# Attention and gated FFN on one core: the bias of 36 steps added by TensorE, their minima by one reduce, and an add moved from ScalarE to GpSimd

## The chip, the cores and the metric

The kernel runs on one core of one Trainium2 chip. A core has TensorE (PE; its weight loads are shown as PEld), VectorE (DVE), ScalarE (ACT), GpSimd (POOL) and SyncE (SP, which here only issues DMAs). Each works through its own queue in order and waits on semaphores of the others. The metric is the device time of one execution in microseconds; lower is better.

## The reference

```python
scores = scale * np.matmul(q, k.transpose(0, 1, 3, 2))          # scale = 1/8
keep = is_global | is_local                                     # 8 global keys, 96 local ones
bias = -slopes[:, None, None] * dist[None, :, :]                # slope 2**-(head+1)
scores = np.where(keep, scores + bias[None], -1e9)
a = np.exp(scores - np.max(scores, axis=-1, keepdims=True))
a = a / (np.sum(a, axis=-1, keepdims=True) + 1e-09)
x = np.matmul(a, v)                                             # B=4, H=8, S=768, D=64
h = np.maximum(x @ w_in, 0.0)                                   # 512 -> 1024
conv = sum(conv_w[t] * shifted(h, t) for t in range(3))
out = (h * (1 / (1 + np.exp(-conv)))) @ w_out                   # 1024 -> 512
```

Only keys inside the window can count, so a tile of 128 queries needs 96 earlier keys, its own 128 and 8 global ones: 232 columns, or 136 for the first tile of a sequence.

## The kernel before

The work is cut into 32 jobs: 4 batches, 2 halves of the sequence (384 queries each), 4 pairs of heads. A job is 3 steps, one for each tile of 128 queries, so there are 96 steps, numbered s = 0 to 95. A step computes both heads of a pair:

- `scores` (L368): q times k on TensorE into PSUM. Jobs 0 to 8 (`NATIVE = 9`, `BESIDE = 9`; steps 0 to 26) multiply in fp32, one head on rows 0 to 63 of the array and the other on rows 64 to 127, line L384. The first head's result goes to a tile named `s`, the second's to one named `sb` from another pool. Later jobs use two split matmuls for each head, line L394, both heads in one bank.
- `maxima` (L402): for each head one DVE instruction, L411, multiplies the scores by -0.125, adds the table `tab` of negated bias and mask (bf16, SBUF), writes the sum back to PSUM and gives its minimum; a short second instruction reads that accumulator.
- `exps` (L416): for each head an Exp on ScalarE with that minimum and a sum, L425. For steps under `SHARED = 40` ScalarE then adds 1e-9 to both sums, L431.
- `normalise` (L433): DVE takes the reciprocals (L437; from step 40 on it also does the add, L436). Up to step 39 GpSimd scales one head (L443) and ScalarE the other (L441).
- `transposes` two steps later (L451, evicted by ScalarE at L453), `values` at the end of a job (L469), and `mixed` (L481, L482), which splits the attention output into two parts for the FFN.

Beside that run: the decode of the weights, which come as 64-bit words, in 16 pieces (DVE L315, L317, L319 and L330, a cast on GpSimd L324, four raw buffers, so a new piece is loaded when an old one has been decoded); the split of q and k for jobs from 9 on (`prep`: casts on GpSimd L136 and L137, subtractions on DVE L140 and L141); and the FFN of the unit before: first matmul `mm1` (L500, L521), convolution (GpSimd L546, DVE L547 and L548), gate, second matmul `mm2` (L611).

Steps 0 to 10 (`HAND = 11`) stand in the order in which the code is written. There DVE gets a budget of decode work for each step, `DECODE_BY_HAND`, later `DECODE_LATER`. From step 11 on a scheduler with a simulated timeline orders each engine's queue, so that an instruction can also be put into a queue's earlier places. Loads of q, k, v and weights share SP's queue. Warm-up matmuls (L169) keep TensorE's clock up in the hand steps.

Of the kernel before, what the change touches and what calls it, by code (L numbers as in the profile page):

```python
# [66 lines left out]
def fast_path(tc, io):  # L67
# [56 lines left out]

    def prep(m, part):
        if m >= len(jobs) or m < NATIVE:
            return
# [243 lines left out]
    def scores(s):  # L371
# [6 lines left out]
        both = ps_s.tile([P, 2, 256], F32, tag="s", name=f"s{s}")  # L378
        sp = [both[:, 0], bank(f"sb{s}", True) if m < BESIDE else both[:, 1]]
        for j in range(2):  # L380
            if m < NATIVE:
# [7 lines left out]
                    stop=True,  # L389
# [3 lines left out]
            for n_, (q_, st, sp_) in enumerate(((qh, True, False), (ql, False, True))):  # L393
# [652 lines left out]
```

## Time and profile before

| | |
|---|---|
| median of 3 runs | 463.97 us (452.75 to 464.49) |
| the profiled execution | 452.65 us, span 450.7 us |
| PE busy | 434.5 us, 96% of the span |
| DVE busy | 351.9 us, 78% |
| ACT busy | 304.0 us, 67% |
| POOL busy | 225.8 us, 50% |
| TensorE's granted clock, mean | 0.995 |

The span runs from the first to the last instruction of the profiled execution. A matmul's duration in the profile holds its way through the array, so the next one starts before it ends, and a busy PE is not a PE at its peak. The same holds in a smaller measure for DVE and ACT: an instruction's shown end can lie behind the next one's start.

### The profile page before, as it was taken

To read this page: it belongs to the slowest core of one execution; us is meant where nothing else is said; L and a number is where in the kernel's file an instruction comes from. 1 tells how busy PE (TensorE), PEld (TensorE's weight loads), DVE (VectorE), ACT (ScalarE), POOL (GpSimd) and SP (SyncE) were. 2 spreads that over 40 slices of the span, in tenths; PEclk is the share of its full clock that TensorE was granted. 3 is DMA by queue.
4 is the path that set the end of the run, shared out by engine and by line. 5 is a ranking of instruction groups with operands and counts; after the bars stand their busy time and mean duration, and the time that the engine had idled before them with its cause. 6 is when DMAs were issued, how large, how long until landed. Compare 5 with 4: busy or idle time off the path is not lost.

```text
span 450.7 us, 9020 instructions
## 1 busy us (share of the span) xinstructions
PE 434.5 (96%) x3027; PEld 375.6 (83%) x3027; DVE 351.9 (78%) x927; ACT 304.0 (67%) x839; POOL 225.8 (50%) x315
## 2 busy tenths in 40 slices
PE   8789999999889999999999999999999999998997
PEld 6555678899768988899989988889989988798876
DVE  6899998889989877757989897847989986447800
ACT  3778878788799667647776576646775696547610
POOL 5654446637835472656675585646675651022000
PEclk9989999999999999999999999999999999999999
DMA  6979941343244332353234333442335223584111
GB/s 213 306 221 275 279 121 43 108 147 105 83 129 150 108 107 97 92 166 107 86 120 160 107 108 91 130 138 81 106 119 163 81 83 119 207 293 132 47 49 52
DMA packets 22662, 60.02 MB, mean 133 GB/s; under 512 B 3024, under 2 KB 5584, under 8 KB 22608
## 3 DMA queue, kind: packets, MB, share of 16 engines
q1 hardware_dynamic: 18992, 53.01, 38.1%
q10 hardware_dynamic: 3616, 6.36, 3.8%
q8 instruction: 26, 0.43, 0.4%
q14 instruction: 28, 0.23, 0.2%
HBM read 53.07 MB, written 6.29 MB: 132 GB/s over the span
## 4 chain that ended last, share of the span: by engine, by line
PE 73%; DVE 5%; ACT 4%; DMA 4%; POOL 2%; issue 2%; ACTq 0%; POOLq 0%; DVEq 0%
PE o L611 24%; PE h L500 24%; PE pv L469 7%; PE t L451 7%; PE s L394 6%; DMA check<-in_w 3%; DVE c L547 1%; PE last L632 1%; POOL pbuf L443 1%; PE sb L384 1%; PE s L384 1%; DVE c L548 1%; DVE c L599 1%; ACT pbuf L425 1%; ACT sat L577 1%
## 5 line engine op out<-in xcount | busy, mean ns | idle before, releaser
L443 POOL TENSOR_SCALAR pbuf<-pbuf,mm 128x232 f32<-128x232 f32 (+1 forms) x152 | 109.1, 726 | 74.1 <-DVE mm L437 49.2
L425 ACT ACTIVATE pbuf<-s,mm 128x232 f32<-128x232 f32 (+1 forms) x165 | 72.5, 444 | 37.6 <-DVE mm L411 22.8
L411 DVE CUSTOM_DVE_ANT_0 s<-s,tab 128x232 f32<-128x232 f32 (+1 forms) x165 | 63.1, 384 | 24.9 <-PE s L394 21.8
L546 POOL TENSOR_SCALAR c<-hbuf,cw 128x382 f32<-128x382 f32 (+1 forms) x64 | 50.0, 786 | 59.3 <-ACT hbuf L510 59.3
L611 PE MATMUL o<-woh,gh 128*128 128x512 f32 x184 | 74.0, 402 | 0.0
L611 PE MATMUL o<-wol,gh 128*128 128x512 f32 x184 | 73.2, 398 | 0.0
L611 PE MATMUL o<-woh,gl 128*128 128x512 f32 x184 | 73.2, 399 | 0.0
L451 PE MATMUL t<-ident,pbuf 128*128 128x128 f32 x384 | 63.0, 278 | 6.6 <-ACT pbuf L441 3.7
L453 ACT ACTIVATE pt<-t 128x512 f32<-128x512 f32 x96 | 58.0, 604 | 15.4 <-PE t L451 15.3
L451 PEld LDWEIGHTS t<-ident,pbuf 128*128 128x128 f32 x384 | 45.5, 141 | 19.6 <-ACT pbuf L441 5.1
L500 PE MATMUL h<-xh,wih 128*128 128x384 f32 x252 | 58.1, 345 | 1.7 <-ACT hbuf L510 1.2
L500 PE MATMUL h<-xl,wih 128*128 128x384 f32 x252 | 58.8, 342 | 0.0
L500 PE MATMUL h<-xh,wil 128*128 128x384 f32 x252 | 56.3, 340 | 0.0
L469 PE MATMUL pv<-pt,v 128*64 128x128 f32 (+1 forms) x768 | 50.0, 279 | 0.3 <-ACT pt L453 0.3
L469 PEld LDWEIGHTS pv<-pt,v 128*64 128x64 f32 (+1 forms) x768 | 42.3, 138 | 8.9 <-issue 2.5
L500 PEld LDWEIGHTS h<-xh,wih 128*128 128x128 f32 x252 | 42.9, 189 | 4.1 <-ACT hbuf L510 1.9
L547 DVE SCALAR_TENSOR_TENSOR c<-hbuf,cw,c 128x382 f32<-128x382 f32 (+1 forms) x64 | 43.7, 697 | 3.0 <-POOL c L546 2.7
L500 PEld LDWEIGHTS h<-xh,wil 128*128 128x128 f32 x252 | 44.2, 189 | 0.3 <-issue 0.3
L500 PEld LDWEIGHTS h<-xl,wih 128*128 128x128 f32 x252 | 44.0, 189 | 0.2 <-issue 0.2
L548 DVE SCALAR_TENSOR_TENSOR c<-hbuf,cw,c 128x382 f32<-128x382 f32 (+1 forms) x64 | 43.4, 686 | 0.3
L510 ACT ACTIVATE hbuf<-h 128x384 f32<-128x384 f32 x64 | 31.9, 500 | 17.4 <-PE h L500 17.0
L611 PEld LDWEIGHTS o<-woh,gl 128*128 128x128 f32 x184 | 34.7, 188 | 7.7 <-issue 0.2
(119 smaller groups left out, 846.6 us busy)
## 6 DMA issues: line engine op xcount, KB each, us to landing
v<-in_vv SPq DMA_DIRECT2D x32, 384.0 KB, 3.7
rq<-in_qk SPq DMA_DIRECT2D x23, 384.0 KB, 3.1
wr<-in_w SPq DMA_DIRECT2D x16, 512.0 KB, 5.2
check<-in_w SPq DMA_DIRECT2D x16, 512.0 KB, 4.6
rk<-in_qk SPq DMA_DIRECT2D x12, 504.0 KB, 3.6
out<-ob ACTq DMA_DIRECT2D x23, 256.0 KB, 2.1
rk<-in_qk SPq DMA_DIRECT2D x11, 408.0 KB, 3.2
rq<-in_qk SPq DMA_DIRECT2D x16, 96.0 KB, 4.4
```

What stands on the lines that cost most here:

```text
L411: last_ttr[s] = V.tensor_tensor_reduce(out=sp[j][:, c0 : c0 + n], in0=sp[j][:, c0 : c0 + n], in1=tb, scale=-0.125, scalar=3.0e38, op0=ALU. ...
L425: last_exp[s] = A.activation(pb[:, j, c0 : c0 + n], sp[j][:, c0 : c0 + n], AF.Exp, bias=mm[:, j : j + 1], scale=-1.0, accum_out=mm[:, 2 + ...
L443: G.tensor_scalar(x, x, inv, 1.0, ALU.mult, ALU.mult)
L451: T.transpose(pt[:, j, c, :], pb[:, j, c * P : (c + 1) * P], ident)
L453: last_ev[s] = A.activation(sb, pt, AF.Copy)
L469: T.matmul(pv[m][64 * j : 64 * j + 64, i * P : (i + 1) * P], vt[m][:n, i, c, 64 * j : 64 * j + 64], sb[:n, j, c, :], start=c == 0, stop=c ...
L500: T.matmul(ps[:, :TB], w_[:, k, fs], x_, start=part == 0 and k == 0, stop=part == 2 and k == NK - 1,)
L510: A.activation(half, ps[:, :TB], AF.Relu, scale=0.5)
L546: G.tensor_scalar(c, *tap(1), 1.0, ALU.mult, ALU.mult)
L547: V.scalar_tensor_tensor(c, *tap(0), c, ALU.mult, ALU.add)
L548: V.scalar_tensor_tensor(c, *tap(2), c, ALU.mult, ALU.add)
L611: last = T.matmul(ps, g_[:, f], w_[:, f], start=f == 0 and part == 0, stop=f == NF - 1 and part == 2,)
```

## The change

Jobs 1 to 12 (`BIASED = (1, 13)`, steps 3 to 38) get their bias from TensorE: after the score matmuls of a head a further one, with a bf16 identity scaled by -0.125 as weights and the table as the moving operand, adds to the same PSUM columns. Since -0.125 is in the weights there, q is multiplied by -0.125 first: for jobs 1 to 8 by a new GpSimd instruction over 128 x 384 in place, for jobs 9 to 12 inside the instructions of `prep`. DVE then takes the minima of both heads with one `tensor_reduce`, which writes nothing back.

For the first 27 steps both heads' scores lie in one tile of two banks (pool `ps_w`, two buffers); at step 27 that pool is given up for the narrow tiles. The add of 1e-9 for steps 0 to 39 is GpSimd's. The decode budgets grow.

```diff
+BIASED = (1, 13)
-DECODE_BY_HAND, DECODE_LATER = (0.3, 1.2, 1.4), (1.2, 1.2)
+DECODE_BY_HAND, DECODE_LATER = (0.3, 1.5, 1.8), (1.6, 1.6)
@@ prep
+        if m < NATIVE and biased(m) and part == 0:
+            q = raw[m][0][:, :TB]
+            G.tensor_scalar(q, q, -0.125, 1.0, ALU.mult, ALU.mult)
...
-            G.tensor_copy(qh, rq)
+            if biased(m):
+                G.tensor_scalar(qh, rq, -0.125, 1.0, ALU.mult, ALU.mult)
+            else:
+                G.tensor_copy(qh, rq)
...
+                V.scalar_tensor_tensor(ql, rq, -0.125, qh.bitcast(F32), ALU.mult, ALU.subtract)
@@ tables
+    A.activation(ident16, ident, AF.Copy, scale=-0.125)
@@ scores
-        both = ps_s.tile([P, 2, 256], F32, tag="s", name=f"s{s}")
-        sp = [both[:, 0], bank(f"sb{s}", True) if m < BESIDE else both[:, 1]]
+        if m < BESIDE:
+            both = wide[1].tile([P, 2, 512], F32, tag="s", name=f"s{s}")
+        else:
+            if not ps_s:
+                narrow()
+            both = ps_s[0].tile([P, 2, 256], F32, tag="s", name=f"s{s}", bufs=2)
+        sp = [both[:, 0], both[:, 1]]
+
+        def bias(j):
+            last_mm[s] = T.matmul(
+                sp[j][:, c0 : c0 + n], ident16, bias_of(s, j), start=False, stop=True
+            )
@@ maxima
+        if biased(m):
+            last_ttr[s] = V.tensor_reduce(
+                mm[:, 0:2], both[:, :, c0 : c0 + n], axis=mybir.AxisListType.X, op=ALU.min,
+            )
+        for j in range(0 if biased(m) else 2):
@@ exps
-        if s < SHARED:
-            A.activation(mm[:, 4:6], mm[:, 2:4], AF.Identity, bias=eps)
@@ normalise
-        if s >= SHARED:
-            V.tensor_scalar(mm[:, 4:6], mm[:, 2:4], 1.0e-9, None, ALU.add)
+        X = G if s < SHARED else V
+        X.tensor_scalar(mm[:, 4:6], mm[:, 2:4], 1.0e-9, 0.0, ALU.add, ALU.add)
```

In the changed program L408 is the bias matmul, L416 the native score matmul, L452 the reduce, L456 the old minimum instruction (other jobs), L479 the add, L480 the reciprocal, L486 the GpSimd scale, L141 the scaling of q, L345 the cast of a weight piece, L494 the transpose, L564 an `h` matmul.

The first place is TensorE's queue at steps 17 and 18, in the part that the scheduler orders; `t` is a transpose, `h` an FFN matmul. Before:

```order
L384 MATMUL s17_850<-rk5_585,rq5_586 128x232
L451 MATMUL t13_792<-ident_153,pbuf1_194 128x128 x4
L384 MATMUL sb17_851<-rk5_585,rq5_586 128x232
L521 MATMUL h0_0_665<-xh3_824,wih_186 128x384
L384 MATMUL s18_887<-rk6_699,rq6_700 128x232
L521 MATMUL h0_0_665<-xl3_825,wih_186 128x384
L521 MATMUL h0_0_665<-xh3_824,wil_187 128x384
L384 MATMUL sb18_888<-rk6_699,rq6_700 128x232
```

And in the changed program:

```order
L416 MATMUL s17_872<-rk5_592,rq5_593 128x232 x2
L408 LDWEIGHTS ident16_158
L408 MATMUL s17_872<-tab_167,ident16_158 128x232
L408 LDWEIGHTS ident16_158
L408 MATMUL s17_872<-tab_167,ident16_158 128x232
L564 MATMUL h0_0_678<-xh3_845,wih_187 128x384
L494 MATMUL t13_814<-ident_153,pbuf1_195 128x128 x4
L564 MATMUL h0_0_678<-xl3_846,wih_187 128x384
L564 MATMUL h0_0_678<-xh3_845,wil_188 128x384
L416 MATMUL s18_912<-rk6_714,rq6_715 128x232 x2
```

The two heads' score matmuls, which had other work between them, now follow each other, and two bias matmuls with their weight loads stand behind them.

The second place is GpSimd's queue at steps 5 to 7, ordered by hand (`mm` holds a step's minima and sums, `pbuf` its exponentials, `w3_0` is a weight piece). Before:

```order
L324 CAST wih_186<-w2_0_379 128x512
L443 TENSOR_SCALAR pbuf2_195<-pbuf2_195,mm5_394 128x232
L324 CAST wih_186<-w3_0_420 128x512
L443 TENSOR_SCALAR pbuf0_193<-pbuf0_193,mm6_447 128x136
L227 TENSOR_SCALAR tab_166<-setup_84 128x368 x2
```

And in the changed program:

```order
L345 CAST wih_187<-w2_0_378 128x512
L479 TENSOR_SCALAR mm5_394<-mm5_394 128x2
L141 TENSOR_SCALAR rq6_715<-rq6_715 128x384
L486 TENSOR_SCALAR pbuf2_196<-pbuf2_196,mm5_394 128x232
L345 CAST wih_187<-w3_0_419 128x512
L141 TENSOR_SCALAR rq3_326<-rq3_326 128x384
L479 TENSOR_SCALAR mm6_447<-mm6_447 128x2
L486 TENSOR_SCALAR pbuf0_194<-pbuf0_194,mm6_447 128x136
```

Each scale now has an add ahead of it, and two scalings of q stand in between, the one of job 6 put in by the scheduler at this early place.

The third is DVE's queue at the same place, in the changed program:

```order
L338 SCALAR_TENSOR_TENSOR w3_0_419<-wr3_0_287,w3_0_419 128x512
L340 SCALAR_TENSOR_TENSOR w3_0_419<-wr3_0_287,w3_0_419 128x512
L452 TENSOR_REDUCE mm7_488<-s7_476 128x2
L480 RECIPROCAL mm6_447<-mm6_447 128x2
L351 TENSOR_TENSOR wil_188<-w2_0_378,wih_187 128x512
L336 TENSOR_SCALAR w0_1_503<-wr0_1_318 128x512
```

The reciprocal of step 6 follows one reduce behind the end of the decode of `w3_0`, and it needs the add that GpSimd has behind the cast of that same piece.

## Rows read from the trace of the kernel before

**Rows 1.** The page's first part: busy time, share of the span, instructions of each engine.

```profile
span 450.7 us, 9020 instructions
PE 434.5 (96%) x3027; PEld 375.6 (83%) x3027; DVE 351.9 (78%) x927; ACT 304.0 (67%) x839; POOL 225.8 (50%) x315
```

**Rows 2.** Busy time of each engine by stretch of the span: stretch and its length, then busy us and instructions of each engine, the granted clock of TensorE, the share of the DMA engines, GB/s.

```profile
11.00:23.00 12.00, 9.26 (x99) 6.55 (x97) 10.86 (x41) 9.52 (x33) 7.97 (x11) 1.00 0.99 306
...
0.00:34.00 34.00, 27.48 (x252) 20.95 (x253) 28.32 (x103) 21.36 (x71) 20.22 (x50) 0.95 0.82 246
34.00:82.00 48.00, 46.98 (x325) 34.66 (x322) 45.49 (x134) 38.37 (x124) 26.04 (x36) 1.00 0.65 189
82.00:97.00 15.00, 14.46 (x107) 13.37 (x108) 12.27 (x32) 12.23 (x38) 8.07 (x10) 1.00 0.30 99
97.00:140.00 43.00, 39.37 (x293) 34.07 (x292) 39.82 (x86) 36.82 (x104) 23.67 (x24) 1.00 0.35 112
140.00:450.70 310.70, 306.20 (x2060) 272.50 (x2058) 225.99 (x576) 195.23 (x506) 147.84 (x198) 1.00 0.36 117
```

**Rows 3.** The chain of waits that ended last, in order of time: start, us on the chain, what ran.

```profile
48.62 0.59 PE s L384 x2
49.21 0.59 PE t L451 x4
49.80 0.59 PE sb L384 x2
...
50.75 0.59 PE s L384 x2
51.34 0.54 PE h L521 x2
51.88 0.59 PE sb L384 x2
...
98.58 1.22 DVE c L599
...
100.69 3.13 DMA rq<-in_qk
...
105.69 1.41 POOL pbuf L443
...
108.07 2.54 POOL pbuf L443 x2
```

**Rows 4.** Instructions in order of time around 31.5 us, step 10: start, us, engine, line, operation.

```profile
31.53 0.46 PE L384 MATMUL s<-rk,rq 64*128 64x232 f32 x1
31.54 0.46 PE L384 MATMUL sb<-rk,rq 64*128 64x232 f32 x1
```

**Rows 5.** The busy time of line L384 alone, by stretch: stretch, its length, PE and PEld busy (instructions), clock, DMA. The first stretch holds steps 0 to 10, the second steps 11 to 26; a step has 4 matmul records.

```profile
0.00:32.30 32.30, 7.20 (x44) 3.95 (x44) 0.95 0.83 251
32.30:82.00 49.70, 17.45 (x64) 8.72 (x64) 1.00 0.64 187
```

**Rows 6.** Groups of instructions by line and shape: line, engine, operation, out<-in, shapes, count | busy us, mean ns of one | idle time before.

```profile
L169 PE MATMUL warm<-setup 128*128 128x128 bf16 x121 | 11.2, 256 | 1.0 <-POOL setup L147 1.0
L411 DVE CUSTOM_DVE_ANT_0 s<-s,tab 128x232 f32<-128x232 f32 x138 | 55.1, 401 | 19.6 <-PE s L394 16.9 <-POOL tab L227 1.2 <-ACT sat L577 0.4
L411 DVE DVE_READ_ACCUMULATOR2_ANT mm<- 128x1 f32 x192 | 26.4, 137 | 0.1
L482 DVE TENSOR_TENSOR xl<-pv,xh 128x384 fp32r<-128x384 f32 x32 | 17.6, 551 | 1.6 <-ACT xh L481 1.3
L443 POOL TENSOR_SCALAR pbuf<-pbuf,mm 128x232 f32<-128x232 f32 x128 | 95.1, 752 | 65.8 <-DVE mm L437 41.6 <-DVE gl L602 4.4 <-ACT pt L453 3.9
L443 POOL TENSOR_SCALAR pbuf<-pbuf,mm 128x136 f32<-128x136 f32 x24 | 14.0, 589 | 8.3 <-DVE mm L437 7.6 <-DVE cw L259 0.5
L285 POOL MEMSET pbuf<- 128x48 f32 x3 | 0.3, 138 | 0.0
L546 POOL TENSOR_SCALAR c<-hbuf,cw 128x382 f32<-128x382 f32 x32 | 24.3, 762 | 18.1 <-ACT hbuf L510 18.1
L324 POOL CAST wih<-w 128x512 fp32r<-128x512 f32 x8 | 6.2, 776 | 3.1 <-DVE w L319 3.1
L441 ACT ACTIVATE pbuf<-pbuf,mm 128x232 f32<-128x232 f32 x32 | 15.9, 497 | 2.7 <-DVE mm L437 2.7
L431 ACT ACTIVATE mm<-mm,misc 128x2 f32<-128x2 f32 x40 | 12.2, 307 | 1.6 <-POOL misc L243 1.2
L425 ACT ACTIVATE pbuf<-s,mm 128x232 f32<-128x232 f32 x138 | 62.4, 458 | 29.6 <-DVE mm L411 14.8 <-PE t L451 8.9 <-DVE mm L437 3.1
```

**Rows 7.** The busy time of line L394 alone after 140 us (columns as in rows 5), and a piece of the chain of waits with twelve `h` matmuls of 384 columns.

```profile
140.00:450.70 310.70, 37.94 (x220) 31.98 (x220) 1.00 0.36 117
...
53.49 2.08 PE h L500 x12
```

**Rows 8.** DVE's instructions in order of time around step 8: start, us, line, operation.

```profile
27.07 0.56 DVE L482 TENSOR_TENSOR xl<-pv,xh 128x384 fp32r<-128x384 f32 x1 [0.47 <-ACT xh L481]
27.54 0.40 DVE L411 CUSTOM_DVE_ANT_0 s<-s,tab 128x232 f32<-128x232 f32 x1
27.86 0.14 DVE L411 DVE_READ_ACCUMULATOR2_ANT mm<- 128x1 f32 x1
27.86 0.44 DVE L411 CUSTOM_DVE_ANT_0 sb<-sb,tab 128x232 f32<-128x232 f32 x1
28.21 0.14 DVE L411 DVE_READ_ACCUMULATOR2_ANT mm<- 128x1 f32 x1
28.21 0.16 DVE L437 RECIPROCAL mm<-mm 128x2 f32<-128x2 f32 x1
```

**Rows 9.** The two loads of job 6's q as SP issues them, the DMA issues by line between 17 and 24 us (count, KB of one, median us from issue to landing), and GpSimd's instructions there with the idle time before them.

```profile
18.76 1.25 SPq L111 DMA_DIRECT2D rq<-in_qk  x2
...
rq<-in_qk SPq DMA_DIRECT2D x3, 96.0 KB, 4.2
...
21.96 0.96 POOL L443 TENSOR_SCALAR pbuf<-pbuf,mm 128x232 f32<-128x232 f32 x1 [0.26 <-DVE setup L262]
24.26 0.61 POOL L324 CAST wih<-w 128x512 fp32r<-128x512 f32 x1 [1.33 <-DVE w L319]
```

**Rows 10.** From the view of line L431, ScalarE's add: who waited for it, us in total, times.

```profile
  DVE mm L437: 2.5, 4
```

More of the change, by code (lines that the diff above doesn't have):

```diff
@@ L82, in fast_path, with narrow @@
     pg = pool("pg", 4)
-    ps_s = pool("ps_s", 2, space=PSUM)
     ps_t = pool("ps_t", 2, space=PSUM)
     ps_v = pool("ps_v", 1, space=PSUM)
-    ps_m = pool("ps_m", 1, space=PSUM)
+    ps_m = {2: pool("ps_m", 1, space=PSUM)}
     p2 = pool("p2", 2)
+    ps_w = tc.tile_pool(name="ps_w", bufs=2, space=PSUM)
+    wide = [ps_w, ps_w.__enter__()]
+    ps_s = []
+    def narrow():
+        wide[0].__exit__(None, None, None)
+        ps = tc.tile_pool(name="ps_s", bufs=1, space=PSUM)
+        ps_s.append(ps.__enter__())
+        ps_m[0] = ps_m[1] = ps_s[0]
+        pools.insert(len(pools) - 1, ps)
     jobs = [(b, u, hp) for b in range(B) for u in range(2) for hp in range(NPAIR)]
@@ L192, in fast_path @@
     make_identity(nc, ident)
+    ident16 = const.tile([P, P], BF16, name="ident16")
     V.tensor_copy(rel, reli)
@@ L240, in fast_path @@
     odd, red, flag = rest[:, 0:3], rest[:, 3:7], rest[:, 7:8].bitcast(I32)
-    bad, ones, ebias, gbias, eps = (rest[:, k : k + 1] for k in range(8, 13))
+    bad, ones, ebias, gbias = (rest[:, k : k + 1] for k in range(8, 12))
     G.memset(gbias, -0.96)
-    G.memset(eps, 1.0e-9)
     def limits():
@@ L388, in scores @@
                     start=True,
-                    stop=True,
+                    stop=not biased(m),
                 )
@@ L392, in scores @@
             qh, ql, kk = qk[m]
-            for n_, (q_, st, sp_) in enumerate(((qh, True, False), (ql, False, True))):
+            for n_, (q_, st, sp_) in enumerate(((qh, True, False), (ql, False, not biased(m)))):
                 last_mm[s] = T.matmul(
@@ L400, in scores, with bias_of @@
                 )
-        st_s[s] = (sp, c0, n, first)
+            if biased(m):
+                bias(j)
+        for j in range(2 if m < NATIVE and biased(m) else 0):
+            bias(j)
+        st_s[s] = (sp, c0, n, both)
+    def bias_of(s, j):
+        m, i = steps[s]
+        b, u, hp = jobs[m]
+        if u == 0 and i == 0:
+            return tab[:, 2 * hp + j, WIN:]
+        return tab[:, 2 * hp + j, 0:WIN]
     def maxima(s):
@@ L405, in maxima @@
         b, u, hp = jobs[m]
-        sp, c0, n, first = st_s[s]
+        sp, c0, n, both = st_s[s]
         mm = p1.tile([P, 8], F32, tag="mm", name=f"mm{s}", bufs=6)
-        for j in range(2):
-            h = 2 * hp + j
-            tb = tab[:, h, WIN:] if first else tab[:, h, 0:WIN]
+        if biased(m):
+            last_ttr[s] = V.tensor_reduce(
+                mm[:, 0:2], both[:, :, c0 : c0 + n], axis=mybir.AxisListType.X, op=ALU.min,
+            )
+        for j in range(0 if biased(m) else 2):
             last_ttr[s] = V.tensor_tensor_reduce(
-                out=sp[j][:, c0 : c0 + n], in0=sp[j][:, c0 : c0 + n], in1=tb,
+                out=sp[j][:, c0 : c0 + n], in0=sp[j][:, c0 : c0 + n], in1=bias_of(s, j),
                 scale=-0.125, scalar=3.0e38, op0=ALU.add, op1=ALU.min,
```

21 lines of the change are left out of this document (11 added, 10 removed).

## The prediction

> **What bounds the kernel now.** I read the page's engine line first [rows 1]. PE is busy 96% of the span, DVE 78%, but those are averages over unlike stages, so the next view is the busy time by stretch [rows 2]. It cuts the run in two. From 140 us on PE is busy 306.20 of 310.70 us, and no instruction of the change lies there. Only the first 140 us can change. In 0 to 34 us PE rests 6.5 us, and once past the start DVE sets the pace, 10.86 of the 12 us from 11 to 23. In 34 to 82 PE is busy 46.98 of 48 and DVE 45.49, so both are close. In 97 to 140 PE rests 3.6 us and DVE 3.2.
>
> Then the chain of waits [rows 3]. Between 48 and 53 us it is PE alone, and the reader is to see one thing in it: the two heads of a step, `s` and `sb`, stand there as separate entries of 0.59 us with a transpose or an `h` matmul between them. Between 98 and 111 us the chain runs through DVE, GpSimd and a DMA; PE is not in it. A gain in the first stretch must come from PE and DVE together; in the second from DVE or GpSimd.
>
> **The heads side by side.** Each head uses 64 of the 128 rows, so the two can run at the same time: in [rows 4] `s` starts at 31.53 and `sb` at 31.54, and both last 0.46. In the 11 steps ordered by hand the line L384 takes 7.20 us, 0.65 a step; in the 16 steps after it, 17.45 us, 1.09 a step [rows 5]. There the two heads lie in tiles that come free at different times, and the scheduler puts other matmuls between them. In the changed program both heads are in one tile and stand next to each other in all 16 steps (the first order listing). If they then run as in the hand steps, PE saves 16 x (1.09 - 0.65) = 7.0 us.
>
> **The bias matmuls.** 36 steps x 2 = 72 more, bf16, mostly 232 columns, each with weights to load. No row shows one. Below: a bf16 warm-up matmul of 128 columns, 11.2 us / 121 = 0.09 us [rows 6]. Above: the split score matmuls, 37.94 us / 220 = 0.17 [rows 7]. The `h` matmuls of 384 columns take 2.08 / 12 = 0.173 [rows 7], by columns 0.105 for 232. I take 0.11, nearest to that one. The 16 scheduled native steps get 32 of them, +3.5 us, on PE's path. Steps 3 to 10 get 16, 1.8 us, hidden by the 6.5 us that PE rests. Jobs 9 to 12 get 24: about 3 steps (0.7 us) before 97 us, where PE is full, on the path; the other 9 steps (2.0 us) lie beside the 3.6 us of rest. If that rest goes they cost their 2.0.
>
> **The minima.** The group rows invite a large saving: 0.401 + 0.137 us for each of two heads [rows 6], 1.08 us a step. The timeline says otherwise [rows 8]: the second head starts 0.32 us after the first (27.54, 27.86) and the reciprocal 0.35 after that; the accumulator reads lie under the next instruction. A step costs 0.67 us. The reduce of 464 columns from PSUM has no row. Nearest below is a 384-column DVE operation from PSUM, 0.551 us with the next instruction starting 0.47 after it (27.07, 27.54) [rows 6, 8]; above, the two that it replaces, 0.67. By columns I take 0.55: 0.12 saved a step, 0 to 0.20 the ends. In 8 hand steps that is 1.0 us on the path. In the next 16 (1.9 us) it only makes room for PE's gain: DVE rests 2.5 us there, and 2.5 + 1.9 = 4.4 covers the 3.5 that PE gives back. In 97 to 140 some 9 steps, 1.1 us, on the path. What is late next is the Exp: the first head's now waits for both heads.
>
> By the Trainium skill (VectorE: DVE Perf Modes, section Rules for kernel authors) `tensor_reduce` on a hot path is the slowest DVE operation and a reason to restructure. Taken as "no cheaper than the two instructions it replaces", it would drop the 2.1 us and leave the sum at 452; rows 8 show no reduce of this size, so it stays open.
>
> **GpSimd's new work.** 40 adds of two columns. Bounds: a 48-column memset, 0.138, and the 136-column scale, 0.589 [rows 6]; I take 0.25, since most of either is fixed cost. ScalarE loses 40 x 0.307 [rows 6]; it is on the chain only in small pieces, and I count 0. Eight scalings of q (128 x 384), near the 382-column tap of `conv` at 0.762 [rows 6], 6.1 us beside GpSimd's idle half. The cost is not the work but the queue. In the second order listing the add for step 6 stands behind the cast of `w3_0` and the scaling of `rq3`. The cast starts only when DVE has finished `w3_0`, and then DVE has one reduce (0.55) before the reciprocal that needs the add. Cast 0.776 (less when undisturbed) + scaling 0.6 to 0.76 + add 0.25 = about 1.7: DVE waits 1.1 us. Where a cast alone is ahead (steps 8 and 5), 0.78 + 0.25 - 0.55 = 0.45 each. Sum +2.0 us, the ends 0 and 4. Behind that wait stand DVE's decode instructions, and the scale and transposes wait with it.
>
> The scaling of `rq6` stands in GpSimd's queue before step 5's scale of `pbuf2`. Before, its two loads are issued from 18.76 to 20.01, 4.2 us to landing, and GpSimd is at that scale at 21.96 [rows 9]: it would wait 1.7 us. Its next cast begins at 24.26 after 1.33 us of idleness, which covers most, so 0 (ends 0 and 2). The loads of `rq7` and `rq8` are alike: 0, ends 0 and 2 each.
>
> **Edits at nothing.** The larger decode budgets move the same 16 weight pieces, whose pace also hangs on DMA at 246 GB/s and a share of 0.82 in the first stretch [rows 2]; without that cover, 2 us either way. `ident16` is one ScalarE instruction before the first Exp. The q of jobs 9 to 12 keeps its instruction count. The wide score tiles take the same four banks, and their exchange at step 27 can cost the wait for one more Exp, 0.458 [rows 6], hidden by `h` matmuls.
>
> **Sum.** -7.0 + 3.5 + 0.7 - 1.0 - 1.1 + 2.0 = -2.9 us. The profiled execution took 452.65 us (span 450.7), so **450 us**. That execution agrees with the lowest of the three runs shown, 452.75; their median, 463.97, is 2.5% above it, and 450 stands 3% below that median.
>
> **Rivals.** (1) *DVE's relief counts in full.* If the accumulator reads do hold DVE, the saving is nearer 2 x 0.538 - 0.63 = 0.45 a step. Then 8 hand steps and 10 late ones give 8.1 us, with PE's -3.5 + 0.7: 452.65 - 10.9 = 441.8, **442**. For it: DVE is the longest in [rows 2] up to 34 us. Against it: the starts in [rows 8]. Chance 0.22.
>
> (2) *GpSimd holds up DVE: slower.* One place, the reciprocal: its input now comes from a queue that also holds casts, q scalings that wait for DMA, and `pbuf` scales of 0.75 us and more. If 16 casts each cost 0.45 (7.2 us), the three late q loads 1.7 each (5.1), and PE waits so that the pairing gives nothing: 452.65 + 7.2 + 5.1 + 0.7 - 2.1 = **463.5**. It decides where the cast, scaling and add last longer than the reduce and whatever DVE does before the reciprocal. For it: GpSimd takes 0.752 for a scale that ScalarE does in 0.497 [rows 6]. Against it: the ScalarE add that it replaces ended only 2.5 us of DVE's waits in 4 times [rows 10], and GpSimd is idle half of the span. Chance 0.16. The Trainium skill (GPSIMD Engine Reference, section Engine selection) puts elementwise adds on VectorE, with one-input operations on GpSimd near line rate; it speaks for this rival's place, and the rows bear out the slower scale.
>
> (3) *The order absorbs it.* The scheduler spreads the freed PE time as other waits and nothing arrives at 140 us: **453**. Chance 0.14. For it: DVE has only 2.5 us to give in 34 to 82.
>
> The forecast itself, 446 to 453, has 0.48.
>
> **Numbers.** Low 441, at rival 1. High 462: rival 2 nearly, and also the upper of the times shown for one and the same kernel, 450 x 1.025 = 461. A measurement of this kernel tells about 2% from no change, 9 us. Faster by more (below 443.6): rival 1 and the forecast's lower edge, 0.27. Within 2%: 0.58. Slower by more: 0.15.
>
> **What would show it.** In the profile after: L416 at about 0.65 us a step in the scheduled native steps too, against 1.09; the bias line at 0.10 to 0.12 us a matmul; the reduce lasting about 0.63 with the next start 0.55 after it; the first `o` matmul or the full-PE stretch starting about 3 us earlier than 140. DVE waiting for the add line by 2 us in all; 8 us or more is rival 2. The forecast is wrong if the stretch after 140 us changes length, or if PE's rest before it grows by more than the pairing gives.

## The result and the profile after

The changed kernel takes **459.67 us** (459.31 to 460.1). The ratio to the kernel before is **1.0147 [1.013, 1.0164]**: 1.5% slower, within the 2% that the forecast called no change. Four of the six runs of the kernel before lie near 464, so the ratio here, and every one below, is taken between undisturbed runs, where before takes about 453. So the sum of the forecast, -2.9 us, should be read against +7.1. The profiled spans, 457.8 against 450.7, differ by the same 7.1.

The engine line of the changed kernel's page, to be read against [rows 1]:

```profile
span 457.8 us, 9148 instructions
PE 435.7 (95%) x3099; PEld 377.4 (82%) x3099; DVE 352.5 (77%) x819; ACT 296.2 (65%) x800; POOL 253.6 (55%) x362
```

PE is busy 435.7 us against 434.5, with 72 matmuls more. Its idle time is span less busy: 457.8 - 435.7 = 22.1 us, before 450.7 - 434.5 = 16.2. So of the 7.1 us, 1.2 are more work on PE and **5.9 are more waiting**.

By stretch, columns as in [rows 2]:

```profile
0.00:34.00 34.00, 26.21 (x244) 19.89 (x245) 24.89 (x71) 17.31 (x56) 21.89 (x58) 0.90 0.77 230
34.00:82.00 48.00, 40.10 (x319) 29.53 (x320) 44.86 (x88) 33.13 (x100) 34.12 (x52) 1.00 0.58 177
82.00:97.00 15.00, 14.51 (x115) 12.61 (x113) 11.94 (x20) 11.95 (x38) 11.16 (x18) 1.00 0.46 136
97.00:140.00 43.00, 43.00 (x328) 39.02 (x328) 36.86 (x56) 34.90 (x96) 31.85 (x37) 1.00 0.32 102
140.00:457.80 317.80, 311.90 (x2100) 276.34 (x2098) 233.99 (x587) 198.87 (x513) 154.61 (x201) 1.00 0.36 117
```

From 34 to 82 us PE now rests 7.9 us where it rested 1.0. From 97 to 140 it is full, 43.00 of 43, where it rested 3.6. What PE did not do early lies there and, 40 instructions more than before, behind 140 us. Up to 34 us DVE's busy time fell from 28.32 us to 24.89, and ScalarE's from 21.36 to 17.31.

Its waits from 0 to 82 us (engine and line waiting, what ended the wait: us in total, times, longest):

```profile
DVE mm L480 <- POOL mm L479: 6.6, 11, 1.1
...
PE t L494 <- POOL pbuf L486: 5.8, 4, 3.2
POOL rq L141 <- DMA rq<-in_qk: 5.6, 3, 3.5
```

The reciprocals wait for GpSimd's add, the scalings of q on GpSimd wait for their loads, and the transposes on PE wait for the scale that stands behind such a scaling. The longest wait on PE in detail: instructions in order of time at steps 5 to 7 (start, us, engine, line, operation, idle time before and what ended it):

```profile
23.25 0.37 PE L408 MATMUL s<-tab,ident 128*128 128x232 bf16 x2
...
23.90 0.17 DVE L480 RECIPROCAL mm<-mm 128x2 f32<-128x2 f32 x1 [0.46 <-POOL mm L479]
...
25.37 0.57 POOL L141 TENSOR_SCALAR rq<-rq 128x384 f32<-128x384 f32 x1 [1.50 <-DMA rq<-in_qk]
...
25.92 0.88 POOL L486 TENSOR_SCALAR pbuf<-pbuf,mm 128x232 f32<-128x232 f32 x1
...
26.85 1.12 PE L494 MATMUL t<-ident,pbuf 128*128 128x128 f32 x4 [3.23 <-POOL pbuf L486]
...
28.17 0.17 DVE L480 RECIPROCAL mm<-mm 128x2 f32<-128x2 f32 x1 [1.15 <-POOL mm L479]
```

The reciprocal of step 5 is done at 24.07, the scale could begin then; it begins at 25.92, since `rq6` ahead of it in GpSimd's queue waits 1.50 us for its load and takes 0.57. PE stands still for 3.23 us. In the same lines stands the wait that the forecast had read out of the order: the reciprocal of step 6 waits 1.15 us for its add, forecast 1.1. Later the chain of waits shows a second one, the same in kind (start, us, what):

```profile
40.83 5.40 DMA rq<-in_qk
...
46.38 0.55 POOL rq L141
...
47.00 0.84 POOL mm L479
...
47.86 0.17 DVE mm L480
48.03 1.02 DVE w L340
49.05 0.55 DVE mm L452
```

A load, the scaling, the add, the reciprocal; and from there to 71 us the chain is DVE and hardly anything else: decode instructions with a reduce between them.

### The profile page after: what moved, and what is told of

The parts are those of the page before. It is cut to its first block, busy times and chain, and to the rows that moved or that the text cites. A ratio compares the mean times of both kernels' runs of the same rounds, so it can differ in the third digit from the quotient of the medians.

```text
span 457.8 us, 9148 instructions
## 1 busy us (share of the span) xinstructions
PE 435.7 (95%) x3099; PEld 377.4 (82%) x3099; DVE 352.5 (77%) x819; ACT 296.2 (65%) x800; POOL 253.6 (55%) x362
## 4 chain that ended last, share of the span: by engine, by line
PE 67%; DVE 13%; DMA 6%; ACT 5%; POOL 4%; issue 3%; SPq 1%; ACTq 0%; POOLq 0%; DVEq 0%
PE o L654 24%; PE h L543 21%; PE pv L512 7%; PE t L494 7%; PE s L426 6%; DMA check<-in_w 3%; DMA rq<-in_qk 2%; DVE c L591 2%; DVE c L590 2%; ACT pbuf L470 2%; DVE mm L452 1%; DVE w L340 1%; PE last L675 1%; DVE w L338 1%; DVE wol L351 1%
## 5 line engine op out<-in xcount | busy, mean ns | idle before, releaser
L486 POOL TENSOR_SCALAR pbuf<-pbuf,mm 128x232 f32<-128x232 f32 (+1 forms) x152 | 109.4, 729 | 71.7 <-DVE mm L480 51.8
L470 ACT ACTIVATE pbuf<-s,mm 128x232 f32<-128x232 f32 (+1 forms) x192 | 84.0, 445 | 51.5 <-DVE mm L456 29.2
L589 POOL TENSOR_SCALAR c<-hbuf,cw 128x382 f32<-128x382 f32 (+1 forms) x64 | 51.0, 801 | 50.1 <-ACT hbuf L553 49.7
L494 PE MATMUL t<-ident,pbuf 128*128 128x128 f32 x384 | 62.5, 279 | 7.6 <-POOL pbuf L486 5.8
L494 PEld LDWEIGHTS t<-ident,pbuf 128*128 128x128 f32 x384 | 46.8, 142 | 17.2 <-POOL pbuf L486 7.4
L456 DVE CUSTOM_DVE_ANT_0 s<-s,tab 128x232 f32<-128x232 f32 (+1 forms) x120 | 46.3, 387 | 18.6 <-PE s L426 16.2
L543 PE MATMUL h<-xh,wil 128*128 128x384 f32 x252 | 57.5, 342 | 0.0
```

What stands on the lines that cost most here:

```text
L456: last_ttr[s] = V.tensor_tensor_reduce(out=sp[j][:, c0 : c0 + n], in0=sp[j][:, c0 : c0 + n], in1=bias_of(s, j), scale=-0.125, scalar=3.0e3 ...
L470: last_exp[s] = A.activation(pb[:, j, c0 : c0 + n], sp[j][:, c0 : c0 + n], AF.Exp, bias=mm[:, j : j + 1], scale=-1.0, accum_out=mm[:, 2 + ...
L486: G.tensor_scalar(x, x, inv, 1.0, ALU.mult, ALU.mult)
L494: T.transpose(pt[:, j, c, :], pb[:, j, c * P : (c + 1) * P], ident)
L543: T.matmul(ps[:, :TB], w_[:, k, fs], x_, start=part == 0 and k == 0, stop=part == 2 and k == NK - 1,)
L589: G.tensor_scalar(c, *tap(1), 1.0, ALU.mult, ALU.mult)
```

## The experiments

All times are medians of the runs that the ratios use, all ratios are against the kernel before. The theories are Q (GpSimd's in-order queue), P (the bias matmuls are work that nothing hides), W (both heads of a step waited for together), and later B (the decode budgets) and C (the clock).

| kernel | what it is | us | ratio [interval] |
|---|---|---|---|
| a_add_act | changed kernel, add back on ScalarE | 456.69 | 1.0094 [1.0065, 1.0122] |
| b_late_q | changed kernel, q scaled later | 462.31 | 1.0211 [1.0166, 1.0257] |
| c_both | a and b | 460.64 | 1.0172 [1.0118, 1.0227] |
| d_wide_only | before, with wide tiles | 453.84 | 1.004 [1.0015, 1.0065] |
| h_late_bias | d, with bias matmuls in jobs 9 to 12 | 460.53 | 1.0191 [1.015, 1.0232] |
| f_add_alone | before, with the add on GpSimd | 456.65 | 1.0091 [1.0069, 1.0114] |
| m_budget_alone | before, with the larger budgets | 456.64 | 1.0088 [1.0064, 1.0112] |
| e_no_q | a, without q scalings | 456.11 | 1.0085 [1.0064, 1.0105] |
| k_noq_all_old | e, with the old budgets | 451.82 | 0.9985 [0.9961, 1.001] |
| g_act_oldbudget | a, with the old budgets | 457.76 | 1.0134 [1.0075, 1.0193] |
| l_after_oldbudget | changed kernel, old budgets | 458.04 | 1.0134 [1.0079, 1.0188] |
| n_noq_hand_old | e, old budgets in the hand steps | 453.82 | 1.0033 [1.0008, 1.0059] |
| o_noq_small | k, smaller budgets | 453.16 | 1.0032 [1.0, 1.0065] |
| j_noq_early_old | k, bias matmuls in jobs 1 to 8 alone | 452.91 | 1.0002 [0.9983, 1.002] |
| p_after_fill | changed kernel, 30 more fillers | 459.97 | 1.0171 [1.014, 1.0201] |
| q_noq_no_fill | k, 28 fillers fewer | 453.49 | 1.0021 [0.9991, 1.005] |
| r_noq_no_add | k, without the add | 450.52 | 0.9946 [0.9923, 0.9969] |
| s_before_no_add | before, without the add | **445.27** | **0.9826 [0.9795, 0.9857]** |

One thing limits what this table can tell. Each edit also changes the order of the queues, because the scheduler orders them anew from about step 9 on: in the pairs compared here about a tenth (GpSimd, PE) to a quarter (DVE) of an engine's instructions up to 140 us then stand in another order. So each difference is the price of a part together with the order that came with it, and no run holds the order fixed. Only up to the reciprocal of step 8 do four of these kernels run the same instructions in the same order on every engine, but for the edit itself. That reciprocal (start, us) in the kernel before, without the add, with the add on GpSimd, and with wide tiles (line numbers are each kernel's own):

```profile
30.48 0.15 DVE L437 RECIPROCAL mm<-mm 128x2 f32<-128x2 f32 x1
...
29.04 0.15 DVE L435 RECIPROCAL mm<-mm 128x2 f32<-128x2 f32 x1
...
31.78 0.17 DVE L435 RECIPROCAL mm<-mm 128x2 f32<-128x2 f32 x1 [0.28 <-POOL mm L434]
...
32.15 0.16 DVE L483 RECIPROCAL mm<-mm 128x2 f32<-128x2 f32 x1
```

By then, in an unchanged order, the add on ScalarE costs 1.44 us, its move to GpSimd 1.30 more (with a stretch at half clock from 13 to 16.5 us that the other three traces lack), and the wide tiles 1.67. In the changed kernel this reciprocal starts at 35.76, 5.28 us late; further on it is 3.3 us late at step 10, 14.2 at step 18 and 7.0 at the last step.

### The add on ScalarE again, and the q scalings moved

a_add_act:

```diff
+        if s < SHARED:
+            A.activation(mm[:, 4:6], mm[:, 2:4], AF.Identity, bias=eps)
...
-        X = G if s < SHARED else V
-        X.tensor_scalar(mm[:, 4:6], mm[:, 2:4], 1.0e-9, 0.0, ALU.add, ALU.add)
+        if s >= SHARED:
+            V.tensor_scalar(mm[:, 4:6], mm[:, 2:4], 1.0e-9, None, ALU.add)
```

> The changed kernel with one part undone: the add of 1e-9 of steps 0 to 39 is ScalarE's again. Theory Q (GpSimd's queue is what costs: the reciprocal waits for the add, 7.1 us of DVE's waits in 12 times, and q scalings that wait for their loads, 5.6 us, hold up what stands behind them): DVE's waits for the add go, the waits for the loads stay and now only delay scales; 455 to 457 us. Theory P (the 72 bias matmuls are the loss, 7.4 us of PE work that nothing hides): no change, 459 to 460. Theory W (the wide score tiles cost, through both heads being waited for together): no change, 459 to 460.

456.69: as Q expected. The add's engine is worth 3.0 us of the 7.1 by the medians, 2.4 by the ratios, with the order that came with it.

b_late_q ties each scaling of q to a step of the job before, so that GpSimd's queue never waits for the load; c_both does this with the add on ScalarE:

```diff
-            G.tensor_scalar(q, q, -0.125, 1.0, ALU.mult, ALU.mult)
...
+            V.tensor_scalar(eighth, mm[:, 0:1], 0.0, -0.125, ALU.mult, ALU.add)
+            G.tensor_scalar(q, q, eighth, 1.0, ALU.mult, ALU.mult)
```

> The changed kernel, but each scaling of q by GpSimd is tied to the minima of the second step of the job before (its factor -0.125 is made on DVE from that step's minimum times zero), so that it can't stand in GpSimd's queue before its load is in; 8 tiny DVE instructions more. The add stays on GpSimd. Theory Q: GpSimd's 5.6 us of waits for loads go, and with them the stops of step 6 and of steps 16 to 18; 454 to 457 us. Theories P and W: 459 to 460.

> Both edits together: the add on ScalarE and the late scalings of q. Theory Q: nearly all of the 7 us comes back, 451 to 454 us. Theory P: 458 to 460, since all bias matmuls stay. Theory W: 458 to 460.

462.31 and 460.64: misses, and a lesson on such experiments. The scaling of job 4's q now comes behind decode work, and the reciprocal of step 12 comes 12 and 8 us later than in the kernel before (53.6 and 49.6 us against 41.2). One wait was exchanged for another, so these two say nothing on the theory. e_no_q below takes the scalings away instead.

### Wide tiles alone

```diff
-BIASED = (1, 13)
+BIASED = (99, 99)
```

with the add on ScalarE and the old budgets.

> The kernel before with one part of the change alone: the wide score tiles, so that the two heads' matmuls follow each other. No bias matmuls (no step is biased), the old minimum instructions, the add on ScalarE, the old decode budgets. Theories Q and P: the pairing is worth up to 7.0 us of PE time where PE is full, so 446 to 450 us. Theory W: the tiles that come free together cost as much as the pairing gives, 452 to 456 us.

453.84, the time that W expected. Its engine line:

```profile
span 451.7 us, 9024 instructions
PE 427.5 (95%) x3027; PEld 371.6 (82%) x3027; DVE 354.6 (78%) x927; ACT 304.6 (67%) x840; POOL 227.4 (50%) x315
```

and its stretch from 34 to 82 us:

```profile
34.00:82.00 48.00, 41.57 (x325) 31.48 (x326) 46.53 (x136) 38.72 (x124) 29.18 (x35) 1.00 0.59 173
```

The reader is to see the whole failure of the forecast's largest term here. The pairing takes 7.0 us off PE (434.5 to 427.5), and the span grows by 1.0, because PE's idle time grows by 8.0 (16.2 to 24.2). In 34 to 82 us PE is busy 41.57 where it was 46.98, and DVE 46.53 of 48 where it was 45.49: DVE sets the pace there. W's own reason, two heads waited for together, is not what the hand steps show. From the first fused minimum instruction of a step to the second it takes 0.48 to 0.61 us on one wide tile, where it took 0.21 to 0.46 on two; over steps 0 to 8 that makes 1.85 us, and d is 1.67 late at step 8.

h_late_bias, that is d with `BIASED = (9, 13)`:

> d_wide_only plus bias matmuls for jobs 9 to 12 alone (24 matmuls of 232 columns, about 2.5 us of PE work; in return one reduce for two fused instructions in 12 steps, and the scaling inside the existing cast of q). No q scaling for jobs 1 to 8, add on ScalarE, old decode budgets. Theory P (PE has no rest left before 140 us, so bias work lands in the end): 455.5 to 457, that is d_wide_only's 453.8 plus 2 to 3. Theory Q (only GpSimd's queue counts): 453 to 454.5, no different from d_wide_only. A gain (DVE is the bound in 97 to 140 and is relieved by 12 x 0.12): 451.5 to 453.

460.53, 3.5 us above the highest expectation. Two of its stretches:

```profile
85.00:90.00 5.00, 0.66 (x5) 0.42 (x5) 3.94 (x6) 3.24 (x11) 2.21 (x2) 1.00 0.14 21
90.00:95.00 5.00, 5.00 (x26) 4.81 (x27) 3.11 (x6) 2.74 (x9) 1.08 (x1) 0.66 0.44 144
```

PE is busy 0.66 of 5 us around the exchange of the wide tiles for narrow ones at step 27, where its score matmul waits 4.34 us for ScalarE's Exp, and works at a clock of 0.66 on the average of the next 5. That is a wait, not 24 matmuls. The forecast had put at most one Exp, 0.458 us, on this exchange, and hidden it; in the changed kernel PE rests 0.5 us there. With bias matmuls in jobs 1 to 8 as well, the late ones cost nothing: j_noq_early_old (k with `BIASED = (1, 9)`) takes 452.91, k 451.82.

> k_noq_all_old with bias matmuls for jobs 1 to 8 alone, jobs 9 to 12 as before the change. Theory P for the late jobs (24 matmuls, 2.5 us on a full PE; h_late_bias was 6.7 above d_wide_only): 446 to 450. If in k_noq_all_old the late bias pays for itself (one reduce in place of two fused instructions, DVE sets the pace in 97 to 140): 452.5 to 454.5. No difference: 451 to 452.5.

So P falls for the late jobs.

### The add alone and the budgets alone

f_add_alone is the kernel before with the two lines of the change for the add, m_budget_alone the kernel before with

```diff
-DECODE_BY_HAND, DECODE_LATER = (0.3, 1.2, 1.4), (1.2, 1.2)
+DECODE_BY_HAND, DECODE_LATER = (0.3, 1.5, 1.8), (1.6, 1.6)
```

> The kernel before with one edit only: the add of 1e-9 to the first 40 steps' sums on GpSimd in place of ScalarE. Theory Q (the add behind casts and scales in GpSimd's queue delays the reciprocal, 3 us in a_add_act against the changed kernel): 454.5 to 457 against 452.5. Rival (the add hurts only together with the q scalings and the larger decode budgets, which crowd GpSimd): 452 to 453.5.

> The kernel before with one edit only: the larger decode budgets. Theory B: 455 to 457.5 against 452.5, DVE work moved ahead delays steps 12 to 20. Rival (the budgets cost only together with the wide tiles, where both heads wait for one reduce): 452 to 454.

456.65 and 456.64: **each alone costs about 4 us**, with no other part of the change present. In f_add_alone the reciprocals (its line L435) wait, us and times:

```profile
its engine sat idle before it (us, times) until:
  POOL mm L434: 5.3, 7
```

Before, it was 2.5 us in 4 times for ScalarE's add [rows 10].

### Without the q scalings, and with the budgets undone

e_no_q is a_add_act with a plain identity as bias weights for the native jobs, maxima, and the 0.125 in Exp:

```diff
-            G.tensor_scalar(q, q, -0.125, 1.0, ALU.mult, ALU.mult)
...
+                op=ALU.max if m < NATIVE else ALU.min,
+            if m < NATIVE:
+                last_ttr[s] = V.tensor_scalar(mm[:, 0:2], mm[:, 0:2], -0.125, 1.0, ALU.mult, ALU.mult)
...
+                scale=0.125 if m < NATIVE and biased(m) else -1.0,
```

> The changed kernel with the add back on ScalarE (as in a_add_act) and with no scaling of q on GpSimd for jobs 1 to 8: the bias weights are a plain identity, the reduce takes maxima, one DVE instruction on two columns turns them into the offset, and Exp carries the 0.125. It costs DVE about 0.06 to 0.1 us more a step (16 steps beyond the hand steps and 8 in them, some 2 us at most). Theory Q (the q scalings wait for loads in GpSimd's queue and hold up what stands behind them: 6.1 us waited 3 times in a_add_act): 452 to 454.5, and the 6.83 us stretch at half clock goes. Theory P (the 72 bias matmuls, 7.4 us of PE work that nothing hides, are what is left): 456 to 458, as a_add_act, plus up to 2 for the added DVE instruction.

k_noq_all_old is e_no_q with the old budgets, g_act_oldbudget is a_add_act with the old budgets, l_after_oldbudget is the changed kernel with the old budgets.

> e_no_q with the old decode budgets (1.2 and 1.4 us a hand step, 1.2 a later step, in place of 1.5, 1.8 and 1.6). Theory B (the larger budgets put decode work of DVE ahead of the steps, so that steps 16 to 21 wait for DVE; they end decoding earlier, at about step 21 against 25, with no gain): 1 to 3 us below e_no_q. Rival (the same pieces have to be decoded anyway, sooner is no loss): within 1 us of e_no_q.

> The changed kernel with the add back on ScalarE and the old decode budgets; the wide tiles, the bias matmuls, the reduce and the q scalings on GpSimd stay. If the parts add up: 452 to 453.5 (k_noq_all_old plus the 0.6 between e_no_q and a_add_act). If the q scalings cost more where the decode does not cover them: 454 to 456.

> The changed kernel with one part undone: the decode budgets as before (1.2 and 1.4 us a hand step, 1.2 a later step, in place of 1.5, 1.8 and 1.6). Theory B (the larger budgets put DVE's decode ahead of the steps where DVE already sets the pace; 4.3 us between e_no_q and k_noq_all_old): 454.5 to 456.5, that is 459.7 less 3 to 5, and the add on GpSimd stays as the rest. Rival (with the add and the q scalings still in GpSimd's queue DVE waits anyway, and the budgets only fill its waits): within 1 us of 459.7.

Measured: e 456.11, k 451.82, g 457.76, l 458.04. With large budgets the q scalings are worth 0.6 us (a against e), with the old ones 5.9 (g against k), but that 5.9 is no wait for a load. By step 18 the two are level (its reciprocal at 57.91 and 57.88 us), and the last scaling of q in g starts at 57.48. What g loses comes later, as in h: PE stops for 3.8 us shortly before step 27, and half clock follows, 0.50 in the column before DMA share:

```profile
82.00:86.00 4.00, 1.24 (x9) 0.96 (x7) 3.97 (x8) 2.01 (x7) 3.17 (x4) 0.97 0.36 134
86.00:92.00 6.00, 4.97 (x20) 4.88 (x20) 3.60 (x7) 4.17 (x12) 2.73 (x4) 0.50 0.43 135
```

Without q scalings the budgets are worth 4.3 (e against k), with them nothing that can be told (a 456.69, g 457.76; l is 1.6 below the changed kernel). So **the parts do not add up**: any one of the add, the q scalings and the budgets, with the order that comes with it, costs 4 to 6 us on a kernel that has none of them, and all three together 7.1 over before, or 7.9 over k. And k, which has the pairing, the bias matmuls and the reduce without those three, is level with the kernel before, though it carries 24 short DVE instructions that the change does not have (4.6 us busy together; where DVE is full the next starts some 0.07 us behind). Its engine line:

```profile
span 448.9 us, 9096 instructions
PE 432.6 (96%) x3099; PEld 375.2 (84%) x3099; DVE 354.5 (79%) x843; ACT 304.5 (68%) x841; POOL 229.0 (51%) x315
```

Its idle PE time, 16.3 us, is that of before: nothing is lost in waits, and nothing won.

n_noq_hand_old and o_noq_small vary the budgets of k further:

> e_no_q with the old budgets in the hand steps alone (1.2 and 1.4), the larger 1.6 in the later steps. If the hand steps matter (the 6.83 us at half clock in e_no_q begin there, at 27 us, and k_noq_all_old has none): 451 to 453, as k_noq_all_old. If the later steps matter (steps 12 to 18 lose 3 us more in e_no_q): 454.5 to 456, as e_no_q. Half each: 453 to 454.5.

> k_noq_all_old with budgets smaller still: 1.0 and 1.2 us a hand step, 1.0 a later step. If less decode beside the first steps goes on helping: 449.5 to 451. If the decoded weights are then late for the first FFN blocks: 453 or more. If 1.2 is flat ground: 451 to 453.

453.82 and 453.16: neither the hand steps nor the later ones alone carry the 4.3, and smaller budgets help no more.

### Is it the clock?

In the changed kernel the clock stands at half from 26 to 32.6 us (0.50 in the column before DMA share is the lower of the two levels, 1.2 GHz of 2.4), and e and k differ in this as well. Stretches of k:

```profile
24.00:26.00 2.00, 1.32 (x12) 0.89 (x12) 1.97 (x5) 1.47 (x5) 0.94 (x2) 1.00 0.36 117
26.00:28.00 2.00, 1.37 (x12) 0.78 (x10) 1.46 (x4) 1.81 (x8) 1.83 (x3) 1.00 0.97 323
28.00:30.00 2.00, 2.00 (x30) 1.61 (x30) 1.97 (x6) 1.32 (x5) 0.86 (x2) 1.00 1.00 232
```

and of e_no_q:

```profile
24.00:26.00 2.00, 1.30 (x12) 0.89 (x12) 1.95 (x5) 1.47 (x4) 0.92 (x2) 1.00 0.53 141
26.00:28.00 2.00, 1.36 (x8) 0.81 (x7) 1.97 (x5) 1.61 (x7) 1.83 (x3) 0.81 0.90 290
28.00:30.00 2.00, 2.00 (x17) 1.35 (x16) 1.97 (x7) 1.21 (x4) 0.88 (x2) 0.50 1.00 224
```

30 PE instructions against 17 in the same 2 us. Two runs change filler matmuls alone. p_after_fill puts 30 ahead of the transposes that wait 3.23 us; q_noq_no_fill takes 28 out of k:

```diff
-WARM_INSIDE = (0, 0, 14, 8, 8)
+WARM_INSIDE = (0, 0, 14, 8, 8, 0, 30)
```

```diff
-WARM = (43, 0, 12, 0, 0, 8, 8, 4, 4, 4, 4, 4)
+WARM = (43, 0, 12, 0, 0, 8, 0, 0, 0, 0, 0, 0)
```

> The changed kernel with 30 more filler matmuls (about 2.7 us at full clock) ahead of step 6's transposes, where PE waits 3.23 us for GpSimd's scale and the clock then falls to half for 6.83 us. Nothing else is changed, no wait is shortened. Theory C (the wait costs by the half clock that follows it): the half-speed stretch there goes or halves and the time falls by 1.7 to 3.4, to 456 to 458. Rival (DVE sets the pace up to 82 us, PE's clock is only a mark): 459 to 460.5.

> k_noq_all_old (451.8, no stretch at half clock in its profile) without the 28 filler matmuls ahead of steps 6 to 11 (2.5 us of PE work that computes nothing). Theory C: one or two stretches at half clock of 3.4 us or more appear between 24 and 45 us, +1.7 to +3.4: 453.5 to 455.5. Rival (PE's clock there costs nothing): 451 to 452.3, or a little faster, since the fillers are gone.

p_after_fill: 459.97, no gain. Its stretches:

```profile
24.00:26.00 2.00, 1.42 (x13) 0.76 (x11) 1.91 (x6) 1.66 (x6) 0.47 (x1) 1.00 0.81 246
26.00:28.00 2.00, 1.02 (x10) 0.91 (x12) 1.15 (x2) 0.35 (x2) 1.96 (x4) 1.00 0.42 82
28.00:30.00 2.00, 1.26 (x8) 0.53 (x7) 1.67 (x4) 1.81 (x7) 1.16 (x3) 0.59 0.89 300
30.00:34.00 4.00, 4.00 (x30) 3.29 (x30) 3.93 (x9) 1.95 (x6) 3.24 (x5) 0.50 0.85 193
...
0.00:82.00 82.00, 69.50 (x590) 53.01 (x591) 69.45 (x158) 50.42 (x158) 54.88 (x109) 0.92 0.68 199
```

The half clock comes 2 us later, not away, and up to 82 us the mean granted clock is lower than in the changed kernel, 0.92 against 0.96; the medians lie 0.3 us apart, and the intervals overlap. Where DVE and the queues set the pace, more half clock cost nothing, and 30 matmuls more cost nothing. In k, where PE has less rest, the fillers' loss gave stretches of 0.57 and 0.66 and 1.7 us:

```profile
28.00:32.00 4.00, 4.00 (x31) 3.38 (x30) 3.90 (x12) 1.91 (x7) 2.65 (x4) 0.57 1.02 280
...
38.00:43.00 5.00, 4.57 (x35) 3.20 (x33) 4.80 (x13) 3.32 (x13) 1.98 (x3) 0.66 0.92 230
```

That is C's lower edge, but the two intervals (0.9991 to 1.005, and 0.9961 to 1.001 of k) touch. So the clock is not the price of the changed kernel; on a kernel without its waits it may be worth some 1.7 us.

The runs on record say the same without an edit. The changed kernel's six have mean clocks from 0.984 to 0.993 and lie within 0.8 us. The kernel before takes 451.3 us at a mean clock of 1.000 (median of 11 runs), 452.5 at 0.996 (31) and 454.2 at 0.992 (10). So for two of the parts the clock is a rival that no run settles. All four runs of f_add_alone stand at 0.984 to 0.989, where the kernel before takes 454.5 to 455.1: some 2 of its 4.1 us may be the clock. And g_act_oldbudget lies at 455.7 and 455.9 (0.989 and 0.991) or at 459.7 and 459.8 (0.981), so its 457.76 is the middle of two values. m_budget_alone shows no such tie: two runs at 0.996 take 456.2 and 456.6, two at 0.989 456.2 and 457.7.

### Without the add at all

```diff
-        if s < SHARED:
-            A.activation(mm[:, 4:6], mm[:, 2:4], AF.Identity, bias=eps)
...
-        V.reciprocal(mm[:, 6:8], mm[:, 4:6])
+        V.reciprocal(mm[:, 6:8], mm[:, 4:6] if s >= SHARED else mm[:, 2:4])
```

> The kernel before without the add of 1e-9 in the first 40 steps, nothing else changed. If the hop itself counts: 449 to 451.5 against 452.5. If it is hidden, and only GpSimd's queue made f_add_alone 4.1 us slower: 452 to 453.

> k_noq_all_old without the add of 1e-9 in the first 40 steps (the sums of a step are at least 1 there, since each row's largest exponent is 0, so that a float32 sum is not changed by it). ScalarE loses 40 x 0.307 us and the reciprocal waits for the Exp alone. If the hop is on the path of the first 20 steps: 447 to 450.5. If DVE and PE set the pace and ScalarE's part lies beside them: 451 to 452.5.

445.27 and 450.52. **The first beats both kernels**: 7.7 us below the kernel before, measured beside it (452.92), and 14.4 below the changed one. It lies 3.7 us under the lowest expectation. Its engine line and its stretch from 34 to 82 us:

```profile
span 444.7 us, 8989 instructions
PE 431.0 (97%) x3027; PEld 373.3 (84%) x3027; DVE 352.2 (79%) x927; ACT 295.1 (66%) x799; POOL 235.3 (53%) x315
```

```profile
34.00:82.00 48.00, 47.39 (x342) 35.93 (x342) 47.85 (x136) 36.96 (x114) 30.18 (x37) 1.00 0.60 181
```

DVE is busy 47.85 of 48 us, against 45.49 [rows 2], and PE's idle time is 13.7 against 16.2. The hop from Exp to an add on another engine to the reciprocal is what the change moved. That it was dear on ScalarE already is shown for the hand steps, 1.44 us by step 8. The other 6.3 us come where the order differs too, and no wait before the reciprocal went: up to 140 us it waits longer for Exp now than it did for the add before, 2.5 us in 4 times [rows 10] (columns as in the waits above):

```profile
DVE mm L435 <- ACT pbuf L425: 3.4, 4, 1.2
```

Hop and order are not told apart there. On k the same edit gains only 1.3 us by the medians, 1.8 by the ratios.

## Why the prediction was wrong, step by step

- **The pairing, -7.0: sized right, placed wrong.** Line L416 alone, by stretch:

```profile
40.00:95.00 55.00, 10.03 (x60) 4.83 (x60) 1.00 0.54 166
```

  60 records are 15 steps: 0.67 us a step, 0.65 forecast. d_wide_only shows the 7.0 us on PE, and that they became waiting. The failing sentence is that DVE's 2.5 us of rest and 1.9 of relief cover PE's gain. The relief was smaller in fact than the new waits, and without it (d) DVE's work grew by 2.7 us (351.9 to 354.6): two fused operations on one wide tile no longer follow each other closely, 1.85 us in steps 0 to 8 alone. In step 0 of the changed kernel the second starts 0.51 us after the first (7.05, 7.56); before, on two tiles, 0.22 (6.53, 6.75).
- **The bias matmuls, +3.5 and +0.7.** From d to the changed kernel PE's busy time grows by 8.2 us for 72 of them, 0.11 each as forecast, though 1.7 of it may be the lower clock up to 34 us (0.90, and 0.95 in d_wide_only). By the sign that the forecast had named, the bias line's own time, it missed: 15.24 us, 0.21 each, not 0.10 to 0.12; that time holds the way through the array. On the path they cost what the reduce gave back: k is level with before.
- **The reduce, -1.0 and -1.1.** It measured as taken:

```profile
L452 DVE TENSOR_REDUCE mm<-s 128x2 f32<-128x464 f32 x29 | 18.1, 629 | 1.9 <-PE s L408 1.8
...
L141 POOL TENSOR_SCALAR rq<-rq 128x384 f32<-128x384 f32 x8 | 4.7, 591 | 5.9 <-DMA rq<-in_qk 5.6 <-PE t L494 0.3
```

  0.63 us, next start 0.55 later (the chain above, 49.05). Rival 1, by which the reduce saves 0.45 a step, did not come: even k, without the three costs below, is level with before, not 11 us faster. The Trainium skill's row on `tensor_reduce` on a hot path, "it's the slowest DVE op. Consider restructuring" (VectorE: DVE Perf Modes, Rules for kernel authors), did not decide here: one reduce was 0.12 us cheaper than the two instructions that it replaced.
- **The add on GpSimd, +2.0.** Mis-sized. The price of the instruction was right (median 0.244 us, though up to 1.247), and so was the one wait read in full (step 6, 1.1 forecast, 1.15 measured); the sum of the waits was not: 7.1 us of DVE in 12 times over the run, 2.4 to 3.0 us of time in this kernel, 4.1 on the kernel before, some 2 of it perhaps the clock. The forecast counted three steps; the waits came in twelve.
- **The q scalings, 0.** The wait was seen (`rq6`, 1.7 forecast, which its own numbers make 1.6 to 2.3 by the load's issue that one counts from; 1.50 measured) and judged by GpSimd's own idle time. It should have been judged by who waits for the instruction behind it: PE's transposes, 3.23 us. What that stop costs in time is not shown. Taking the scalings out gains 0.6 us with the large budgets, and with the old ones 4.0 or 7.9, by which of g's two values is taken; that loss comes after the last scaling, from a stop shortly before step 27 and the half clock behind it.
- **The budgets, 0, within 2 either way.** +4.0 to 4.4 alone, 1.36 of it by step 8 (31.84 us against 30.48). The cover named, DMA's pace, did not hold; the decode instructions stand ahead of reduces on DVE, the engine that sets the pace.
- **ScalarE's relief, 0.** The 2.5 us in [rows 10] misled: without the add the kernel before gains 7.7. In the hand steps, where the order is the same, the hop cost 1.44 us in nine steps; the rest is hop and order together.
- **The rivals.** Rival 2 came, at 459.7 for its 463.5, and in the main by its mechanism: a reciprocal behind casts, q scalings that wait for DMA, PE waiting so that the pairing gives nothing. Its 0.16 was far too low: of three costs of the same sign two were set at 0 and one at the middle of its bounds, and the add and the budgets came out at or beyond the upper end. It lacked the budgets. The bound of 8 us of DVE waiting that was to show it was nearly met, 7.1.
- **The stretch behind 140 us** was to stay the same length. It grew by 7.1 us, with 40 more PE instructions: work put off from before, not a change of its own.

What stays open: how much of each price is the order that came with the edit, and why three costs of 4 to 6 us make 7.1 together. p_after_fill gives a reason that fits, but was not tested further: once DVE waits, PE has 8 us of rest in 34 to 82 us, in which a second cost of the same kind disappears. Why removing the add gains 7.7 on before and 1.3 on k is open too, as is whether b's edit with another place for the scaling would have helped.

## What to carry to other kernels

Work freed on an engine is worth nothing where another engine sets the pace; look first whether that one gets relief in the same stretch, and from what. An instruction that moves to an in-order queue costs what waits behind it, so ask of each instruction ahead of it whether it can wait for a transfer. And before moving a small operation that stands between two engines, ask whether it is needed at all: taking it out gained 1.7%, moving it lost 0.9%. Where a scheduler orders the queues, read what an edit does in the part whose order stayed the same, and call the rest part and order together.

## What the hardware showed that was not expected

- e_no_q and k_noq_all_old keep PE busy alike up to 28 us, within 0.02 us in each of the stretches shown; one falls to half clock in 26 to 28, the other does not fall at all. What PE was seen to do before does not tell them apart here. The same holds within one kernel: of k's ten runs five have a mean clock of 1.000 and five of 0.996.
- An add of 128 x 2 on GpSimd took 0.222 to 1.247 us, median 0.244: it can take five times its usual time, and it stands before DVE's reciprocal.
